# A fused GEGLU kernel: x of the second half transposed ahead of its use and kept in DRAM, wd sums staged in the pairs alone

## The chip, the cores and the metric

One core of a Trainium2 chip runs the whole kernel. The metric is the device time of one execution in microseconds, as the median over runs; lower is better. The kernel before takes 554.97 us (12 runs, 553.82 to 557.05).

## What is computed

The inputs are `x` (1 x 2048 x 1024), `w_gate` and `w_up` (1024 x 3584) and `w_down` (3584 x 1024), all bf16; the output is bf16.

```python
def reference(x, w_gate, w_up, w_down):
    return (_gelu(x @ w_gate) * (x @ w_up)) @ w_down   # gelu: tanh form
```

## The kernel before

The 2048 rows of x are worked off in two halves of 1024 rows (`h` = 0 and 1). Each half has a gate and up stage, which fills `hT` (the products, transposed, 28 f tiles of 128), and a down stage of two groups of 512 rows.

Most matrix products are not done plainly. Two by two blocks are multiplied in seven products instead of eight, from sums of blocks (a Strassen-Winograd scheme). In the gate and up stage, a *pair* (`pair_quads`) takes two f tiles and the half's two row blocks: its seven products, each for gate and up, are called m1, m5, m6, m2, m3 and two that are named by their sums s4 and a22, in this order, with 8 matmuls each, 56 in all. They need sums of x blocks (`t_sum`: t1, t2, t3, b22, t4, in `t_mem`, once in a half) and sums of weight blocks (`s_sum`, L350 on GpSimd, made for the next pair while the present one runs, in `s_mem`). Between the products VectorE adds (`add_m5`, L399) and multiplies gelu and up (`mult`, L255, which writes `hT`), and ScalarE copies banks and takes gelu. The first 512 columns of f of the first half are done plainly instead, in eight *units* (`first_units`, `unit`, L232). After the units come twelve pairs in the first half (pairs 2 to 13) and fourteen in the second. Weights of gate and up lie in two buffers of 512 columns each; `load_w` (L155) fills the next one at the start of every even pair, when the pair before has left it.

In the down stage (`down_group`), each of the four groups does seven products in the order m1, m5, m6, m7, m2, m3, m4 (28 matmuls each, L600). Their right side needs sums of blocks of w_down. t1 and t3 are made on VectorE from loaded rows, b22 on ScalarE, and t2 and t4 come ready from DRAM (`t_dram`, loaded at L520 in 512 KB pieces, as slots in `t_mem` come free). These two were *staged*: during the first half's gate and up stage, `stage_load` (L534) loads two rows of tiles of w_down into `wd_sb` (three buffers), and `stage_sums` makes three subtractions on VectorE (L548) into three `o_sb` tiles and stores two of them to `t_dram` (L552). There are 14 such steps. `o_sb` has four buffers. The b21 blocks are loaded at L496.

x must lie transposed in SBUF (`xT`, one buffer). The first half's is made on TensorE (first 512 rows) and by one DMA transpose (L172, `load_xT`). The second half's is loaded in the first half's down stage by 16 DMA transposes of 512 rows x 128 columns (128 KB each): six and four in group 0 behind m5 and m6, six in group 1 behind m5. In group 1 `w_fill` (L830) also brings the second half's first weights.

What sets the order: the helpers `sp`, `act`, `dve`, `pool`, `pe` tie each instruction to the one before it on its engine, so every engine runs in the order of the program text. Nearly all DMAs are issued by SyncE (`sp`), in one queue; a DMA that must wait there holds those behind it. Where `then["m2"]` and the like are filled, the listed work is issued behind that product of the pair or group. The lines that place the staging before:

```python
            stage_load(0)
            stage_load(1)
            unit(hT, (0, 0), 0, 1)
...
            for fi in range(1, FPG):
                stage_sums(fi - 1)
                stage_load(fi + 1)
                unit(hT, (0, 0), fi, 1)
...
                if i + 2 < NS:
                    then["m2"] = [lambda i=i: stage_load(i + 2)]
                if i < NS:
                    then["m4"] = [lambda i=i: stage_sums(i)]
```

Of the kernel before, what the change touches and what calls it, by code (L numbers as in the profile page):

```python
# [10 lines left out]
BF16 = mybir.dt.bfloat16  # L11
# [20 lines left out]
def kernel(  # L32
# [8 lines left out]
    nc = tc.nc  # L41
    P = 128
# [4 lines left out]
    KD = D // P  # L47
    KH = KD // 2
    KF = F // P
    TB = 512  # L50
    NH = 2
    SH = S // NH
    NTB = SH // TB
    FG = 512
    FPG = FG // P
# [6 lines left out]
    WKP = 2  # L62
# [5 lines left out]
    NS = KF // 2  # L68
# [5 lines left out]
    xv = x2.rearrange("t (ko ki) -> t ko ki", ki=P)  # L74
# [10 lines left out]
    o_pool = ctx.enter_context(tc.tile_pool(name="o", bufs=4))  # L85
    dram_pool = ctx.enter_context(
        tc.tile_pool(name="dram", bufs=1, space=bass.MemoryType.DRAM)
    )
# [11 lines left out]
    assert NR * DN == 5 * KH * TB and NS - 4 >= 2 * KD // 2  # L100

    t_dram = dram_pool.tile([P, 2, NS, DN], F32, name="t_dram")

    banks = [psum.tile([P, TB], F32, name=f"bank{i}") for i in range(8)]
    PB, VB, QB, RB = (0, 1), (2, 3), (4, 5), (6, 7)
# [18 lines left out]
    def sp(inst):  # L124
        return on("sp", inst)
# [43 lines left out]
    def load_xT(xT, h, tb, k0, k1):  # L169
        t0 = h * SH + tb * TB  # L170
        sp(
            nc.sync.dma_start_transpose(  # L172
                out=xT[:, k0:k1, tb * TB : (tb + 1) * TB],
                in_=xv[t0 : t0 + TB, k0:k1, :],
            )
        )
# [353 lines left out]
    def stage_load(i):  # L530
        w = wd_pool.tile([P, WDT, D], BF16, name="wd_sb")
        for j in range(2):
            k = j * NS + i
            sp(nc.sync.dma_start(out=w[:, j : j + 1, :], in_=wdv[:, k : k + 1, :]))  # L534
        staged[i] = w

    def stage_sums(i):
        w = staged[i]

        tt = [o_pool.tile([P, DN], F32R, name="o_sb") for _ in range(3)]  # L540
        ops = (
            (w[:, 0, DN:D], w[:, 0, 0:DN]),
            (w[:, 1, DN:D], tt[0][:].bitcast(F32)),
            (w[:, 1, 0:DN], tt[1][:].bitcast(F32)),
        )
        for t, (in0, in1) in zip(tt, ops):
            dve(
                nc.vector.tensor_tensor(out=t[:], in0=in0, in1=in1, op=ALU.subtract)  # L548
            )
        for j in range(2):  # L550
            sp(
                nc.sync.dma_start(  # L552
                    out=t_dram[:, j, i, :], in_=tt[1 + j][:].bitcast(F32)
                )
            )

    def s_down(hT, grp, name, i0, i1):
        n = 0 if name in ("s1", "s2", "s4") else 1
        for i in range(i0, i1, 2):
            t = left(n, i, i + 2)  # L560

            def a(l, j):
                c0 = grp * TB + l * 2 * P
                return hT[:, j * NS + i : j * NS + i + 2, c0 : c0 + 2 * P]

            if name == "a22":
                act(nc.scalar.copy(out=t, in_=a(1, 1)))
                continue
            in0, in1, op = {
                "s1": lambda: (a(1, 0), a(1, 1), ALU.add),  # L570
                "s2": lambda: (t.bitcast(F32), a(0, 0), ALU.subtract),
                "s3": lambda: (a(0, 0), a(1, 0), ALU.subtract),
                "s4": lambda: (a(0, 1), t.bitcast(F32), ALU.subtract),
            }[name]()
            dve(nc.vector.tensor_tensor(out=t, in0=in0, in1=in1, op=op))  # L575
# [167 lines left out]
    for h in range(NH):  # L743
        hT = hT_pool.tile([P, KF, SH], BF16, name="hT")
        first_pair = 0
        if h == 0:
            first_units(hT)
            t_sum("t2")
            for fi in range(NSU, FPG):
                unit(hT, (0, 0), fi, 0)  # L750
            t_sum("b22")
            t_sum("t3")
            stage_load(0)
            stage_load(1)
            unit(hT, (0, 0), 0, 1)
            for name in S_NAMES:
                for j in range(2):
                    s_sum(0, PPG, j, name)
            t_sum("t4")
            for fi in range(1, FPG):  # L760
                stage_sums(fi - 1)
                stage_load(fi + 1)
                unit(hT, (0, 0), fi, 1)
            first_pair = PPG
        for pair in range(first_pair, NPAIR):
            if pair % PPG == 0 and (pair // PPG + 1) * PPG < NPAIR:
                key = (h, pair // PPG + 1)
                if key not in chunks:
                    new_chunk(key)
                    load_w(key, 0, KD, nc.sync)  # L770
            then = {}
            if h == 0:
                i = pair - first_pair + FPG - 1
                if i + 2 < NS:
                    then["m2"] = [lambda i=i: stage_load(i + 2)]
                if i < NS:
                    then["m4"] = [lambda i=i: stage_sums(i)]
            if pair == NPAIR - 2:

                load_wd_rows(0, 4)  # L780
                load_wd_rows(4, 8)
            if 6 < pair < 11:
                i = 2 * pair - 8
                then["m3"] = [lambda i=i: s_down(hT, 0, "s3", i, i + 2)]
            if pair == NPAIR - 1:
                load_b22(4, 10)
                load_b22(10, NS)
                then |= {
                    "m5": [lambda: s_down(hT, 0, "s1", 0, 4)],
                    "m6": [lambda: s_down(hT, 0, "s1", 4, 8)],  # L790
                    "m2": [
                        lambda: load_wd_rows(8, 10),
                        lambda: load_wd_rows(10, 12),
                        lambda: load_wd_rows(12, NS),
                        lambda: load_b22(0, 4),
                    ],
                    "m7": [lambda: t_down(0, "t1", 0, 2)],
                    "m3": [lambda: t_down(0, "t1", 2, 4)],
                    "m4": [
                        lambda: t_down(0, "t2", 0, NT2),  # L800
                        lambda: t_down(0, "t1", 4, 8),
                        lambda: s_down(hT, 0, "s1", 8, NS),
                        lambda: t_down(0, "t1", 8, NS),
                    ],
                }
            pair_quads(
                hT, h, pair, (h, pair + 1) if pair + 1 < NPAIR else None, then
            )

        then0 = {"m5": [lambda: s_down(hT, 0, "s3", 0, 6)]}  # L810
        then1 = {}
        if h + 1 < NH:
            nh = h + 1
            xT = xT_pool.tile([P, KD, SH], BF16, name="xT")
            slices = [(tb, kd) for tb in range(NTB) for kd in range(KD)]

            def x_fill(n):
                fs = []
                for _ in range(n):
                    tb, kd = slices.pop(0)  # L820
                    fs.append(lambda tb=tb, kd=kd: load_xT(xT, nh, tb, kd, kd + 1))
                return fs

            def w_fill(c, j):
                if j == 0:
                    new_chunk((nh, c))
                w_sb, wv = chunks[(nh, c)][j], (wgv, wuv)[j]
                for k0 in range(0, KD, KH):
                    src = wv[:, k0 : k0 + KH, c * FG : (c + 1) * FG]
                    sp(nc.sync.dma_start(out=w_sb[:, k0 : k0 + KH, :], in_=src))  # L830

            def s_fill(j, *names):
                for name in names:
                    s_sum(nh, 0, j, name, True)

            then0["m5"] += x_fill(6)
            then0["m6"] = x_fill(4)
            then1["m5"] = x_fill(6)
            then1["m6"] = [lambda: w_fill(0, 0)]
            then1["m7"] = [lambda: w_fill(0, 1)]  # L840
            then1["m3"] = [
                lambda: t_sum("t1"),
                lambda: s_fill(0, "s1", "s2"),
                lambda: s_fill(1, "s1", "s2"),
            ]
            then1["m4"] = [
                lambda: s_fill(0, "a22"),
                lambda: s_fill(1, "a22"),
                lambda: t_sum("b22"),
                lambda: t_sum("t2"),  # L850
                lambda: t_sum("t3"),
                lambda: s_fill(0, "s3"),
                lambda: s_fill(1, "s3"),
                lambda: s_fill(0, "s4"),
                lambda: s_fill(1, "s4"),
                lambda: t_sum("t4"),
                lambda: [w_fill(1, j) for j in range(2)],
            ]
        for grp, then in enumerate((then0, then1)):
            down_group(hT, h, grp, then)  # L860
# [30 lines left out]
```

## Time and profile before

| what | value |
|---|---|
| median of 12 runs | 554.97 us |
| the profiled execution's own time | 554.39 us |
| its span | 552.6 us |
| TensorE busy | 540.2 us, 98% |
| VectorE, ScalarE, GpSimd busy | 350.6, 259.6, 243.6 us |
| DMA moved | 100.61 MB, mean 182 GB/s |
| units and start, to the first pair | 0 to 35.66 us |
| pairs of the first half | 35.66 to 193.28 us |
| its down groups | 193.28 to 239.60 to 284.68 us |
| pairs of the second half | 284.68 to 461.08 us |
| its down groups | 461.08 to 505.03 to about 549.1 us |

The profile is of one execution. PE is TensorE, DVE is VectorE, ACT is ScalarE, POOL is GpSimd, SPq is SyncE's queue of DMA issues; L376 is line 376 of the kernel. A row of a group of instructions ends with the engine's idle time ahead of them and what ended most of it, behind an arrow. A row in order of time begins with its start and its length, both in us; matmuls overlap, so a start and a length may reach into the next row. A row of a stretch has its bounds, its length, then busy time and number of instructions of PE, weight loads, DVE, ACT and POOL, then the clock that TensorE was granted (1.00 is full), the share of time that the DMA engines were busy, and the GB/s that they moved. "To landing" is the time from a DMA's issue until its data is there.

### The profile page before, as it was taken

The page shows a single profiled execution, that of the slowest core. Times are in us where ns is not written, and L with a number is a line of the kernel's source. Part 1 is how long each engine was busy: PE and PEld are TensorE (multiplying, and loading weights), DVE is VectorE, ACT ScalarE, POOL GpSimd, SP SyncE. Part 2 cuts the span into 40 slices and gives each one's busy share as a digit, 9 for nine tenths or more (in the row PEclk, how much of TensorE's full clock was granted, in tenths as well). Part 3 has the DMA queues.
Part 4 walks back from the last instruction along what each step waited for, and adds up shares of the span by engine and source line. Part 5 has one row for each costly group of instructions (what it writes and reads, how often), then busy time and mean ns, then how long its engine had stood idle before and what let it go on. Part 6 is the DMA issues. An engine that isn't in the chain of part 4 may idle for free.

```text
span 552.6 us, 7231 instructions
## 1 busy us (share of the span) xinstructions
PE 540.2 (98%) x2409; PEld 374.2 (68%) x2409; DVE 350.6 (63%) x465; ACT 259.6 (47%) x434; POOL 243.6 (44%) x206
## 2 busy tenths in 40 slices
PE   8969999999999999999999999999999999999997
PEld 4426677767777767658666777776777666866865
DVE  1893665566666899779394444444444459979861
ACT  2414555555555516313655555555555552361270
POOL 0476667777777000000019777777677740000000
PEclk9998999999999999999999999999999999999999
DMA  9848272737435689869990404224040447867846
GB/s 274 259 146 273 77 230 100 251 98 238 134 134 188 230 301 222 273 223 315 316 348 1 152 20 133 87 67 148 5 153 0 154 131 237 279 198 258 282 143 204
DMA packets 78788, 100.61 MB, mean 182 GB/s; under 512 B 16288, under 2 KB 60832, under 8 KB 78752
## 3 DMA queue, kind: packets, MB, share of 16 engines
q1 hardware_dynamic: 78208, 99.63, 55.9%
q10 hardware_dynamic: 544, 0.52, 0.3%
q8 instruction: 19, 0.31, 0.2%
q14 instruction: 17, 0.14, 0.1%
HBM read 85.46 MB, written 11.53 MB: 176 GB/s over the span
## 4 chain that ended last, share of the span: by engine, by line
PE 92%; DMA 5%; DVE 2%; issue 0%; SPq 0%; ACT 0%; ACTq 0%; DVEq 0%
PE bank L376 59%; PE bank L600 29%; DMA t_mem<-t_dram 3%; PE bank L232 3%; DMA w_mem<-in_w_up_dram 1%; DVE o_sb L548 1%; DMA wd_sb<-in_w_down_dram 1%; DVE t_mem L226 0%; DVE hT L255 0%; PE bank L294 0%; ACT o_sb L648 0%; ACTq L155 0%; SPq L534 0%; SPq L552 0%; DVEq L548 0%
## 5 line engine op out<-in xcount | busy, mean ns | idle before, releaser
L376 PE MATMUL bank<-t_mem,s_mem 128*128 128x512 f32 x1040 | 256.2, 401 | 0.0
L376 PEld LDWEIGHTS bank<-t_mem,s_mem 128*128 128x128 f32 x1040 | 196.3, 189 | 45.6 <-issue 0.3
L350 POOL TENSOR_TENSOR s_mem<-w_mem 128x512 fp32r<-128x512 bf16 x100 | 123.0, 1251 | 204.5 <-PE bank L376 185.1
L600 PE MATMUL bank<-t_mem,s_mem 128*128 128x512 f32 x560 | 131.6, 394 | 2.0 <-DMA t_mem<-t_dram 1.8
L399 DVE TENSOR_TENSOR bank<-bank,m 128x512 f32<-128x512 f32 x104 | 72.3, 699 | 93.0 <-ACT bank L419 83.7
L600 PEld LDWEIGHTS bank<-t_mem,s_mem 128*128 128x128 f32 x560 | 104.7, 188 | 26.7 <-issue 4.4
L376 PE MATMUL bank<-xT,w_mem 128*128 128x512 bf16 x416 | 99.8, 383 | 4.6 <-DVE hT L255 4.6
L255 DVE TENSOR_TENSOR hT<-w_mem,bank 128x512 bf16<-128x512 f32 x104 | 71.3, 687 | 50.5 <-ACT w_mem L250 26.3
L250 ACT ACTIVATE w_mem<-bank 128x512 f32<-128x512 f32 x104 | 61.7, 596 | 79.5 <-DVE bank L399 46.0
L376 PEld LDWEIGHTS <-w_mem 128*128 128x128 bf16 x416 | 36.6, 98 | 55.6 <-issue 18.8
L525 DVE TENSOR_TENSOR t_mem<-w_mem 128x1024 fp32r<-128x1024 bf16 x56 | 65.5, 1217 | 0.0
L350 POOL TENSOR_TENSOR s_mem<-w_mem,s_mem 128x512 fp32r<-128x512 bf16 x50 | 62.7, 1274 | 0.0
L350 POOL TENSOR_TENSOR s_mem<-s_mem,w_mem 128x512 fp32r<-128x512 f32 x50 | 59.4, 1211 | 0.0
L363 ACT CAST s_mem<-w_mem 128x512 fp32r<-128x512 bf16 x52 | 31.9, 615 | 29.9 <-PE bank L376 29.2
L575 DVE TENSOR_TENSOR s_mem<-hT 128x512 fp32r<-128x512 bf16 x56 | 36.6, 685 | 9.1 <-PE bank L600 7.0
L600 PEld LDWEIGHTS <-hT 128*128 128x128 bf16 x224 | 21.2, 98 | 26.7 <-issue 2.1
L414 ACT COPY m<-bank 128x512 f32<-128x512 f32 x52 | 30.6, 588 | 17.9 <-PE bank L376 17.8
L410 ACT COPY bank<-bank 128x512 f32<-128x512 f32 x52 | 29.5, 571 | 19.0 <-PE bank L376 19.0
L419 ACT COPY bank<-bank 128x512 f32<-128x512 f32 x52 | 29.6, 570 | 17.1 <-PE bank L376 17.1
L648 ACT CAST o_sb<-bank 128x512 bf16<-128x512 f32 x28 | 15.3, 584 | 42.4 <-PE bank L600 30.4
L232 PE MATMUL bank<-xT,w_mem 128*128 128x512 bf16 x128 | 28.1, 379 | 0.4 <-DMA w_mem<-in_w_up_dram 0.2
L522 ACT CAST t_mem<-w_mem 128x1024 fp32r<-128x1024 bf16 x28 | 26.9, 1047 | 0.0
(37 smaller groups left out, 225.5 us busy)
## 6 DMA issues: line engine op xcount, KB each, us to landing
t_mem<-t_dram SPq DMA_DIRECT2D x56, 512.0 KB, 5.9
w_mem<-in_w_gate_dram SPq DMA_DIRECT2D x11, 1024.0 KB, 5.6
w_mem<-in_w_up_dram SPq DMA_DIRECT2D x11, 1024.0 KB, 8.1
wd_sb<-in_w_down_dram SPq DMA_DIRECT2D x28, 256.0 KB, 5.6
t_dram<-o_sb SPq DMA_DIRECT2D x28, 256.0 KB, 2.1
wd_sb<-in_w_down_dram SPq DMA_DIRECT2D x12, 512.0 KB, 8.7
w_mem<-in_w_down_dram SPq DMA_DIRECT2D x10, 512.0 KB, 6.6
w_mem<-in_w_down_dram SPq DMA_DIRECT2D x4, 1024.0 KB, 7.1
```

The lines of the kernel that those rows point to most:

```text
L232: return nc.tensor.matmul(ps[:], lhsT=w_sb[:, kd, fi * P : (fi + 1) * P], rhs=xT[:, kd, tb * TB : (tb + 1) * TB], start=(kd == 0), stop=(k ...
L250: act(nc.scalar.activation(out=g_sb, in_=ps[:], func=ACT.Gelu_apprx_tanh))
L255: nc.vector.tensor_tensor(out=hT[:, fc, tb * TB : (tb + 1) * TB], in0=g_sb, in1=ps[:], op=ALU.mult,)
L350: pool(nc.gpsimd.tensor_tensor(out=t, in0=in0, in1=in1, op=op))
L363: act(nc.scalar.copy(out=t, in_=a(1, 1)))
L376: nc.tensor.matmul(banks[bank][:], lhsT=lhs[:, c, :], rhs=rhs[:, c, :], start=start and c == 0, stop=c == KH - 1, skip_group_check=True,)
L399: nc.vector.tensor_tensor(out=banks[dst][:], in0=banks[src][:], in1=m5[j][:], op=ALU.add)
L414: act(nc.scalar.copy(out=m5[j][:], in_=banks[VB[j]][:]))
L419: act(nc.scalar.copy(out=banks[RB[j]][:], in_=banks[QB[j]][:]))
L525: dve(nc.vector.tensor_tensor(out=t, in0=in0, in1=in1, op=ALU.subtract))
L575: dve(nc.vector.tensor_tensor(out=t, in0=in0, in1=in1, op=op))
L600: nc.tensor.matmul(banks[bset[u]][:], lhsT=lhs(i, u), rhs=rhs(i), start=start and i == 0, stop=stop and i == NS - 1, skip_group_check=True,)
```

## The change

It has three parts. The 14 staging steps no longer begin in the units: step 0 is loaded at their end, and the steps run behind pairs 2 to 12, four in every three pairs, so that behind some pairs two steps follow each other. In pairs 2 to 9, behind m5, two pieces of the second half's x are transposed by DMA into an `o_sb` tile each and stored to a new tensor in DRAM, `x_dram` (`stage_x`). In the down stage of the first half the 16 transposes are gone; behind m6 of group 0, four plain loads of 512 KB bring `xT` from `x_dram`.

```diff
+    x_dram = dram_pool.tile([P, KD, SH], BF16, name="x_dram")
...
+    def stage_x(tb, kd):
+        t0 = SH + tb * TB
+        t = o_pool.tile([P, 1, TB], BF16, name="o_sb")
+        sp(
+            nc.sync.dma_start_transpose(
+                out=t[:], in_=xv[t0 : t0 + TB, kd : kd + 1, :]
+            )
+        )
+        sp(
+            nc.sync.dma_start(
+                out=x_dram[:, kd : kd + 1, tb * TB : (tb + 1) * TB], in_=t[:]
+            )
+        )
...
-            stage_load(0)
-            stage_load(1)
             unit(hT, (0, 0), 0, 1)
...
             for fi in range(1, FPG):
-                stage_sums(fi - 1)
-                stage_load(fi + 1)
                 unit(hT, (0, 0), fi, 1)
             first_pair = PPG
+            xs = [(tb, kd) for tb in range(NTB) for kd in range(KD)]
+            stage_load(0)
...
             if h == 0:
-                i = pair - first_pair + FPG - 1
-                if i + 2 < NS:
-                    then["m2"] = [lambda i=i: stage_load(i + 2)]
-                if i < NS:
-                    then["m4"] = [lambda i=i: stage_sums(i)]
+                at = [min((pair - first_pair + d) * 4 // 3, NS) for d in range(3)]
+                then["m5"] = [lambda q=q: stage_x(*q) for q in xs[:2]]
+                xs = xs[2:]
+                then["m2"] = [lambda i=i: stage_load(i) for i in range(at[1], at[2])]
+                then["m4"] = [lambda i=i: stage_sums(i) for i in range(at[0], at[1])]
...
-            def x_fill(n):
-                fs = []
-                for _ in range(n):
-                    tb, kd = slices.pop(0)
-                    fs.append(lambda tb=tb, kd=kd: load_xT(xT, nh, tb, kd, kd + 1))
-                return fs
+            def x_fill(k0, k1):
+                src = x_dram[:, k0:k1, :]
+                sp(nc.sync.dma_start(out=xT[:, k0:k1, :], in_=src))
...
-            then0["m5"] += x_fill(6)
-            then0["m6"] = x_fill(4)
-            then1["m5"] = x_fill(6)
+            then0["m6"] = [
+                lambda k0=k0: x_fill(k0, k0 + WKP) for k0 in range(0, KD, WKP)
+            ]
```

More of the change, by code (lines that the diff above doesn't have):

```diff
@@ L814 @@
             xT = xT_pool.tile([P, KD, SH], BF16, name="xT")
-            slices = [(tb, kd) for tb in range(NTB) for kd in range(KD)]
-            def x_fill(n):
-                fs = []
-                for _ in range(n):
-                    tb, kd = slices.pop(0)
-                    fs.append(lambda tb=tb, kd=kd: load_xT(xT, nh, tb, kd, kd + 1))
-                return fs
+            def x_fill(k0, k1):
+                src = x_dram[:, k0:k1, :]
+                sp(nc.sync.dma_start(out=xT[:, k0:k1, :], in_=src))
             def w_fill(c, j):
```

## The prediction

> **What bounds the kernel now.** I read the page first (busy shares and clock), then TensorE's order of time, then VectorE around TensorE's one long gap, then SyncE's queue and the two down stages beside each other.
>
> ```profile
> PE 540.2 (98%) x2409; PEld 374.2 (68%) x2409; DVE 350.6 (63%) x465; ACT 259.6 (47%) x434; POOL 243.6 (44%) x206
> ...
> PEclk9998999999999999999999999999999999999999
> ...
> L600 PE MATMUL bank<-t_mem,s_mem 128*128 128x512 f32 x560 | 131.6, 394 | 2.0 <-DMA t_mem<-t_dram 1.8
> ...
> L376 PE MATMUL bank<-xT,w_mem 128*128 128x512 bf16 x416 | 99.8, 383 | 4.6 <-DVE hT L255 4.6
> ```
>
> TensorE is the bound. Only what stops it or slows its clock can be won, and the page names two such places: 4.6 us ahead of a gate/up matmul, and 1.8 us of t loads in the down stages. The dip in the clock row (fourth slice, 41 to 55 us) stands right behind the first. This is VectorE there, and the clock in four stretches:
>
> ```profile
> 28.56 1.64 DVE L548 TENSOR_TENSOR o_sb<-wd_sb 128x512 fp32r<-128x512 bf16 x1
> 30.23 3.09 DVE L548 TENSOR_TENSOR o_sb<-wd_sb,o_sb 128x512 fp32r<-128x512 bf16 x2
> 33.24 0.67 DVE L255 TENSOR_TENSOR hT<-w_mem,bank 128x512 bf16<-128x512 f32 x1
> ...
> 40.59 0.68 DVE L255 TENSOR_TENSOR hT<-w_mem,bank 128x512 bf16<-128x512 f32 x1
> ```
> ```profile
> 36.70:41.30 4.60, 0.00 (x0) 0.00 (x0) 4.50 (x6) 0.57 (x1) 0.78 (x1) 1.00 0.61 199
> 41.30:43.20 1.90, 1.88 (x5) 0.94 (x5) 0.00 (x0) 0.00 (x0) 0.00 (x0) 0.51 1.05 383
> 43.20:45.50 2.30, 2.30 (x8) 1.78 (x8) 0.00 (x0) 1.15 (x2) 0.54 (x1) 0.67 1.02 325
> 54.70:67.30 12.60, 12.60 (x58) 8.92 (x58) 7.53 (x11) 6.87 (x13) 9.21 (x9) 1.00 0.25 84
> ```
>
> Nine wd sums (L548), 1.5 us each while GpSimd works beside them, stand between the products (L255) of the last four plain units. The last product, which frees the bank of the first pair's second matmul group, comes at 40.59 instead of at about 35.9. TensorE stands from 36.7 to 41.3, and comes back at clock 0.51, then 0.67. An undisturbed pair takes 12.60 us; this first one takes 19.02 (35.66 to 54.68).
>
> The down stages, from SyncE's queue and TensorE:
>
> ```profile
> 206.39 17.41 SPq L172 DMA_TRANSPOSE xT<-in_x_dram  x10
> 223.92 1.46 SPq L520 DMA_DIRECT2D t_mem<-t_dram  x3
> ...
> 253.01 10.41 SPq L172 DMA_TRANSPOSE xT<-in_x_dram  x6
> ...
> 484.61 2.14 SPq L520 DMA_DIRECT2D t_mem<-t_dram  x3
> ```
> ```profile
> 234.15 2.18 PE L600 MATMUL bank<-t_mem,s_mem 128*128 128x512 f32 x7 [0.39 <-DMA t_mem<-t_dram]
> 237.90 1.86 PE L600 MATMUL bank<-t_mem,s_mem 128*128 128x512 f32 x7 [0.53 <-DMA t_mem<-t_dram]
> 283.00 1.84 PE L600 MATMUL bank<-t_mem,s_mem 128*128 128x512 f32 x7 [0.56 <-DMA t_mem<-t_dram]
> ```
>
> The ten transposes hold SyncE until 223.8, so the first t4 loads go out 30.6 us after their group began (193.28); in the same group of the second half, without transposes, 23.5 us after (461.08 to 484.61). From TensorE's order of time the four groups last 46.32, 45.08, 43.95 and about 44.0 us. The first half's two are 2.4 and 1.1 us longer, though one program text does all four.
>
> **The change, part by part.**
>
> *The sums leave the unit stage.* VectorE then has, behind the last t sum (26.18, 2.45 us), only products of 0.67 us, each ready when its unit's matmuls end. The last unit's end at 35.8, so its product is done at about 36.6, where TensorE asks at 36.55. The first pair costs 12.60 + 0.1 instead of 19.02: **−6.3 us**. What could be next late: GpSimd's s4 sums for that pair end at 37.46 and are needed 9 us after its start; weights of chunk 1 landed before 24. Neither waits. If the clock did not recover with the gap, only the 4.6 would be won. A rule of the Trainium skill bears on that (TensorE: Matmul & The Clock Gate, Part 1: The HAM clock gate): the half clock comes after some 3.4 us of idleness and needs about as long to go. The trace agrees (4.63 us of idleness; 0.51 and 0.67 until 45.5), so gap and slow clock go together: 4.6 by the gap alone, 6.3 with both; I take 6.3. The gaps of 0.33 to 0.56 us in the down stages stand at clock 1.00.
>
> *The transposes leave the down stages.* Group 0: SyncE issues the b21 loads to 206.35, then four loads of x of 512 KB, about 0.5 us of queue each, done by about 209, against 223.8. Their 2 MB follow 1.75 MB of b21; at 289 to 335 GB/s (these stretches' rates) both are through by about 217, when the first t4 loads may go (193.28 + 23.5). So group 0 falls to the second half's 43.95: **−2.3 us** (bounds 0 and −2.4). Group 1: w_fill's gate loads waited behind the transposes till 263.53; their slots are free when the t3 sums end at 260.3, so they go 3.2 us earlier. The last t4 load (issued 274.67, landed 8.2 us later) sat behind some 5.75 MB issued from 263.5 on, and was 0.56 us late; 3 us less backlog removes the wait: **−1.0** (bounds 0 and −1.1).
>
> *Sixteen transposes and stores enter the pairs.* Per pair, in eight pairs, SyncE's queue gets: transpose, store, transpose, store. A store waits for its transpose to land, and behind it stand the next transpose, the wd loads (L534) and the stores of the sums (L552). No row shows a transpose in the pairs. From the rows: standing alone one lands 2.7 us after issue (the last of the ten), 4.0 in the median of the 17, and 9.0 behind 1.75 MB, namely 0.5 after what was ahead of it; a store is 0.33 of queue and lands in 2.0. I take 2.7, and 0.5 behind a backlog, since in a pair each transpose stands alone but for the weights. Queue time over two pairs, 25.2 us: weights issued to first transpose landed 0.55 + 7.9 + 0.5 = 9.0; the other three transposes 9.0 (2.7 to 3.2 each); four stores 1.4; wd loads 2.5 (2.67 tiles of 0.95); stores of sums 2.0: 23.9. It fits, with 1.3 to spare. With 4.0 for the three it is 27, and the queue slips 2 us each two pairs.
>
> Here a rule speaks against the change (DMA: Bandwidth & Descriptors, Rules for kernel authors): make transfers of 1 MiB or more and join small ones. The trace's one large transpose (1 MB, landed in 8.1 us) beside eight small at 2.7 gives 21.6: joined pieces would need 16 us in all and no store between. By the row 16 × (2.7 + 0.35) = 49 us of queue are spent, but over 101 us of pairs in which SyncE now mostly waits for VectorE. The rule would price it at a slip; I keep the row's sum.
>
> *Who waits for a slip.* VectorE writes sums into the four o_sb slots that the transposes use too. Where a pair ends with two sums (first behind pair 4), the fifth of the six subtractions needs the slot of the second transpose, so its store must have landed. With P the start of pair 5: weights go out at 3.6 us into pair 4 (stores of the sums before end there), first transpose landed P + 0.1, store, second transpose P + 0.45 to 3.15, store issued 3.2, landed P + 5.25. Sums run from P + 1.05 (55.73 − 54.68) and would reach that one at 3.85; it starts at 5.3, both are done at 6.7, then add_m5 (L399) to 7.4. It starts at P + 5.34 today, and TensorE needs it only at P + 8.9 (s4 follows 40 matmuls). Margin 1.5 us, cost nothing; without that cover each later us is TensorE's. In the other even pairs the third subtraction needs the first transpose's store, about P + 2 to 4.5, limit P + 7.5. Weights may come 4 us later without GpSimd waiting: they land 9 and 12.2 us after the pair's start, it starts on them 15.5 after, and it is idle 3.4 of 12.6. Bounds of this part: 0 and +10; I take **+0.2**. A gain is excluded, since TensorE stands nowhere in these pairs.
>
> *The sums' new rate* (14 in 11 pairs): two sums are 4.2 us from P + 1.05, ending at 5.25 against the add's 5.34: nothing. Store and load of x are 4 MB more; DMA share in the pairs is 0.25 and 0.75: hidden.
>
> Sum: −6.3 − 2.3 − 1.0 + 0.2 = **−9.4 us**. The profiled execution took 554.39 (span 552.6), 0.6 below the median of 554.97: 545.0, and as a median **545.6**.
>
> **The rivals.** (A) *SyncE slips, a part is given back.* At 4.0 us a transpose the slip is 2 us each two pairs, 6 to 8 by the last transposes; after margins of 1.5 to 3 TensorE loses 2 to 6 us: 547.5 to 551.5. For it: the 4.0 median, the 9.0. Against it: that median comes from ones issued 1.3 us apart. Chance 0.22. (B) *Slower.* The same queue, in pairs 4 to 9: when those three transposes take 5 us each, two pairs' queue work is 30 us, the slip 4.7 each two pairs and 19 over the eight, less the margin of 3: 554.97 − 9.6 + 16 = 561. It decides from about 4.6 us per transpose (slip 3.4, 14 over the eight, less 3: 11), well above the 2.7 of the row. Chance 0.07. (C) *The down stages keep their waits* (x's 2 MB loads delay b21 or t4 as the transposes did): only −6.3 comes, 548.7. Against it: the same groups of the second half, and the idle DMA there. Chance 0.06. (D) *Nothing shows*, slips and gains equal, 555: 0.03. That it doesn't do what it says has no room: the built order has the transposes ahead of the wd loads and no L548 among the units.
>
> **How the numbers follow.** The likeliest case, 0.62, gives 544.6 to 546.8. The range goes to 550.5, into A, and leaves out B, D and A's end. Faster by over 0.2% (about what a measurement of this kernel can tell from no change) is the main case, A and C: 0.90; same 0.03; slower 0.07.
>
> **What would show it.** Right: no gap ahead of the first pair's second group, clock 1.00 from slice two on, pair 2 lasting 12.6 to 12.7; down groups of 44.0 and 44.1; the x transposes landing in 2.7, or 8 to 9 behind weights; L548's waits on DMA below 3 us each. Wrong: L399 ending waits of TensorE in pairs 5, 8 or 9, with VectorE waiting for x_dram<-o_sb (A, B), or t_mem<-t_dram still ending waits at L600 (C).

## The result, and the profile after

| | before | changed |
|---|---|---|
| median | 555.15 us (47 runs, 553.30 to 557.13) | 551.79 us (11 runs, 547.17 to 553.14) |
| ratio to before | | 0.992 (0.991 to 0.994) |
| the profiled execution, its span | 554.39, 552.6 us | 550.14, 548.1 us |

The change gains 3.4 us, where 9.4 were forecast (545.6), and lands above the range's upper end, 550.5. In a second set of runs the same kernel took 549.49 us (548.91 to 551.05; 0.990, 0.989 to 0.992). The lines of the page of the changed kernel that answer to those of before (the same code has other line numbers now: L548 is L549, L399 is L400, L376 is L377, L600 is L616):

```profile
PE 539.6 (98%) x2409; PEld 374.7 (68%) x2409; DVE 355.9 (65%) x465; ACT 259.3 (47%) x434; POOL 244.0 (45%) x206
...
PEclk9999999999999999999999999999999999999999
...
L377 PE MATMUL bank<-t_mem,s_mem 128*128 128x512 f32 x1040 | 255.9, 400 | 3.5 <-DVE bank L400 3.5
...
L616 PE MATMUL bank<-t_mem,s_mem 128*128 128x512 f32 x560 | 130.1, 393 | 0.0
...
L377 PE MATMUL bank<-xT,w_mem 128*128 128x512 bf16 x416 | 99.0, 381 | 0.0
```

Both waits named before are gone: L616 (down stages) stands 0.0, and so does the gate/up row that lost 4.6. The clock row has no dip left. But a third row has a wait that it did not have: 3.5 us for VectorE's add (L400). TensorE's order of time says where, as its last bracket (idle time ahead, and what ended it):

```profile
123.88 3.91 PE L377 MATMUL bank<-t_mem,s_mem 128*128 128x512 f32 x16 [2.08 <-DVE bank L400]
...
289.04 3.93 PE L377 MATMUL bank<-t_mem,s_mem 128*128 128x512 f32 x16 [1.39 <-DVE bank L400]
```

Those are the s4 products of pair 8 of the first half and of the first pair of the second half. From the same view, stage by stage:

| stage | before | changed | difference | forecast |
|---|---|---|---|---|
| start and units, to the first pair | 35.66 | 36.91 | +1.25 | 0 |
| first pair (pair 2) | 19.02 | 12.76 | −6.26 | −6.3 |
| pairs 3 to 13 | 138.60 | 140.96 | +2.36 | +0.2 |
| down group 0 | 46.32 | 43.94 | −2.38 | −2.3 |
| down group 1 | 45.08 | 43.95 | −1.13 | −1.0 |
| first pair of the second half | 12.60 | 14.29 | +1.69 | 0 |

The sum is −4.47, and the spans differ by 4.5. The gains all came at their forecast size (−9.77 against −9.6); the loss is three places that were priced at next to nothing. The first of them is the start: there the first 16 small transposes on TensorE took 1.89 us in this execution against 1.07 before. The second profile of the same kernel has 1.07 and reached its first pair at 35.55, and 1.89 comes again in two of the variants below, so that term belongs to the execution and not to the change.

**Pair 8** (its start P is 112.67). SyncE's queue in the pair before it; start, length of issuing, and what goes where:

```profile
106.54 1.88 SPq L535 DMA_DIRECT2D wd_sb<-in_w_down_dram  x4
...
109.41 1.98 SPq L563 DMA_TRANSPOSE o_sb<-in_x_dram  x1
114.50 0.32 SPq L568 DMA_DIRECT2D x_dram<-o_sb  x1
114.86 1.12 SPq L563 DMA_TRANSPOSE o_sb<-in_x_dram  x1
117.44 0.32 SPq L568 DMA_DIRECT2D x_dram<-o_sb  x1
```

Pair 6 issued the weights at 91.75, and its own first transpose, behind them, landed 11.4 us later (9.0 forecast). So the queue reaches pair 7's transposes late, and behind four wd loads (1 MB). The first lands 5.1 us after issue (109.41 to the store at 114.50), the second 2.6, and its store goes out only at P + 4.8. VectorE and GpSimd meanwhile:

```profile
116.36 0.92 DVE L549 TENSOR_TENSOR o_sb<-wd_sb,o_sb 128x512 fp32r<-128x512 bf16 x1 [1.24 <-DMA x_dram<-o_sb]
...
119.30 0.69 DVE L549 TENSOR_TENSOR o_sb<-wd_sb 128x512 fp32r<-128x512 bf16 x1 [2.02 <-DMA x_dram<-o_sb]
120.03 3.10 DVE L549 TENSOR_TENSOR o_sb<-wd_sb,o_sb 128x512 fp32r<-128x512 bf16 x2
120.98 3.16 POOL L351 TENSOR_TENSOR s_mem<-w_mem 128x512 fp32r<-128x512 bf16 x2
123.05 1.28 DVE L400 TENSOR_TENSOR bank<-bank,m 128x512 f32<-128x512 f32 x2
```

Two subtractions wait 1.24 and 2.02 us for the stores of x to give their slots back. The last two then take 1.55 us each, not 0.7, since GpSimd's sums run at the same time. The add starts at P + 10.4; TensorE's gap of 2.08 says that P + 8.3 was the latest that costs nothing. With 0.7 for the two it would have been 1.7 us earlier, a gap of some 0.4 (an estimate); without the 3.26 of waiting, in time: in the run without transposes, below, it starts at P + 7.8.

**First pair of the second half** (P is 278.52):

```profile
281.42 3.23 POOL L351 TENSOR_TENSOR s_mem<-w_mem 128x512 fp32r<-128x512 bf16 x2 [103.13 <-PE bank L377]
282.00 3.21 DVE L349 TENSOR_TENSOR s_mem<-w_mem,s_mem 128x512 fp32r<-128x512 bf16 x2
285.13 3.24 DVE L227 TENSOR_TENSOR t_mem<-xT,t_mem 128x2048 fp32r<-128x2048 bf16 x1
288.30 1.28 DVE L400 TENSOR_TENSOR bank<-bank,m 128x512 f32<-128x512 f32 x2
```

VectorE makes this half's first sums in one chain without idle time (t1, s1, s2, t2, t3, s3, s4, t4), which starts inside group 1. Before, it started 8.14 us ahead of the pair; the t4 waits of group 1 lay behind that start, so TensorE's waiting gave VectorE time. Now it starts 7.00 ahead. GpSimd's first sums for the next pair begin at P + 2.9 as ever, so in both kernels the chain's last pieces fall beside them. Before (P is 284.68), they began while VectorE was at s4, and it was GpSimd that waited:

```profile
287.01 1.28 DVE L348 TENSOR_TENSOR s_mem<-w_mem,s_mem 128x512 fp32r<-128x512 bf16 x2
287.58 5.05 POOL L350 TENSOR_TENSOR s_mem<-w_mem 128x512 fp32r<-128x512 bf16 x2 [106.64 <-PE bank L376]
288.22 2.28 DVE L226 TENSOR_TENSOR t_mem<-xT,t_mem 128x2048 fp32r<-128x2048 bf16 x1
```

Now they begin while VectorE is still at s3, and the two take turns: s4 takes 3.21 for two (1.28 before), t4 3.24 (2.28 before). No run here shows what settles who waits. 1.14 + 1.93 + 0.96 = 4.0 later: the add starts at P + 9.8 where it started at P + 5.7, and TensorE stands 1.39.

### The profile page after: what moved, and what is told of

Its sections match the earlier page's. It is cut to its first block, busy times and chain, and to the rows that moved or that the text cites. A ratio compares the mean times of both kernels' runs of the same rounds, so it can differ in the third digit from the quotient of the medians.

```text
span 548.1 us, 7258 instructions
## 1 busy us (share of the span) xinstructions
PE 539.6 (98%) x2409; PEld 374.7 (68%) x2409; DVE 355.9 (65%) x465; ACT 259.3 (47%) x434; POOL 244.0 (45%) x206
## 4 chain that ended last, share of the span: by engine, by line
PE 92%; DMA 4%; DVE 3%; issue 1%; SPq 0%; ACT 0%; DVEq 0%; ACTq 0%
PE bank L377 56%; PE bank L616 30%; PE bank L233 5%; DMA o_sb<-in_x_dram 1%; DVE s_mem L349 1%; DMA out_dram<-o_sb 1%; DMA w_mem<-in_x_dram 1%; PE bank L295 1%; DVE t_mem L222 0%; DVE o_sb L549 0%; DVE t_mem L224 0%; DVE bank L400 0%; DMA x_dram<-o_sb 0%; DVE t_mem L227 0%; ACT o_sb L664 0%
## 5 line engine op out<-in xcount | busy, mean ns | idle before, releaser
L377 PE MATMUL bank<-t_mem,s_mem 128*128 128x512 f32 x1040 | 255.9, 400 | 3.5 <-DVE bank L400 3.5
L377 PEld LDWEIGHTS bank<-t_mem,s_mem 128*128 128x128 f32 x1040 | 195.4, 188 | 49.4 <-issue 2.5
L351 POOL TENSOR_TENSOR s_mem<-w_mem 128x512 fp32r<-128x512 bf16 x100 | 119.3, 1213 | 198.7 <-PE bank L377 171.6
L616 PE MATMUL bank<-t_mem,s_mem 128*128 128x512 f32 x560 | 130.1, 393 | 0.0
L400 DVE TENSOR_TENSOR bank<-bank,m 128x512 f32<-128x512 f32 x104 | 71.6, 696 | 77.6 <-ACT bank L420 69.6
L616 PEld LDWEIGHTS bank<-t_mem,s_mem 128*128 128x128 f32 x560 | 105.2, 188 | 22.7
L377 PE MATMUL bank<-xT,w_mem 128*128 128x512 bf16 x416 | 99.0, 381 | 0.0
L377 PEld LDWEIGHTS <-w_mem 128*128 128x128 bf16 x416 | 36.5, 98 | 50.6 <-issue 13.4
L351 POOL TENSOR_TENSOR s_mem<-s_mem,w_mem 128x512 fp32r<-128x512 f32 x50 | 65.4, 1329 | 0.0
L351 POOL TENSOR_TENSOR s_mem<-w_mem,s_mem 128x512 fp32r<-128x512 bf16 x50 | 60.8, 1236 | 1.1 <-PE bank L377 1.1
L616 PEld LDWEIGHTS <-hT 128*128 128x128 bf16 x224 | 21.2, 98 | 26.7 <-issue 2.1
L549 DVE TENSOR_TENSOR o_sb<-wd_sb,o_sb 128x512 fp32r<-128x512 bf16 x28 | 24.6, 879 | 6.3 <-DMA x_dram<-o_sb 5.4
```

The lines of the kernel that those rows point to most:

```text
L351: pool(nc.gpsimd.tensor_tensor(out=t, in0=in0, in1=in1, op=op))
L377: nc.tensor.matmul(banks[bank][:], lhsT=lhs[:, c, :], rhs=rhs[:, c, :], start=start and c == 0, stop=c == KH - 1, skip_group_check=True,)
L400: nc.vector.tensor_tensor(out=banks[dst][:], in0=banks[src][:], in1=m5[j][:], op=ALU.add)
L616: nc.tensor.matmul(banks[bset[u]][:], lhsT=lhs(i, u), rhs=rhs(i), start=start and i == 0, stop=stop and i == NS - 1, skip_group_check=True,)
```

## The experiments

The theory behind them (Q): a slip of SyncE's queue reaches VectorE and, in pair 8, TensorE. Its rival (R): four steps in three pairs are too much for VectorE by themselves, since two sums behind one pair do not fit beside GpSimd. The kernel before took 555.1 to 555.7 us beside them.

**The changed kernel once more**, and with each half of it taken away. No edit in the first.

> The changed kernel once more. Its first profile (550.14 us) has two new waits of TensorE for add_m5 on VectorE: 2.08 us behind the two sums that follow pair 7, and 1.39 us in the second half's first pair; its granted clock is 1.000. Most other runs are 551 to 553 at a clock of 0.997. Theory Q (the queue slips, and sums that come late are slow) and rival R (two sums behind one pair are too much for VectorE whatever the queue does) both expect 551.8 +- 0.7 again. If the runs at 0.997 differ by a longer wait and a slow clock behind it, a profile at 0.997 shows a gap of over 2.1 us with clock near 0.5 behind it, worth some 1.7 us; if it is the start, the first pair begins later than at 36.9 instead.

549.49 us. Its profiled execution (550.38 us) shows the gap of pair 8 at another cost. Two stretches of it (columns as explained with the profile before):

```profile
120.02:123.44 3.42, 1.36 (x6) 0.86 (x5) 3.39 (x6) 0.00 (x0) 2.71 (x2) 1.00 0.56 199
123.44:126.85 3.41, 3.41 (x9) 2.64 (x8) 3.31 (x6) 1.08 (x2) 2.33 (x2) 0.50 0.99 322
```

TensorE stands 2.06 us (120.41 to 122.47), all of it within the first stretch, and through the next it has half the clock: the 16 matmuls behind the gap take 5.49 us. In the first profile of the changed kernel they took 3.91 behind a gap of 2.08 (121.80 to 123.88):

```profile
122.14:125.55 3.41, 1.67 (x7) 1.43 (x8) 3.41 (x6) 0.00 (x0) 2.36 (x3) 1.00 0.68 209
125.55:128.97 3.42, 3.42 (x17) 2.14 (x16) 3.31 (x6) 2.92 (x6) 1.96 (x2) 1.00 1.04 354
```

So the same gap costs 2.1 or 3.7 us. The bounds of these stretches are not chosen freely. In every profile here the half clock behind a gap lasts 3.41 us (twice that in one, the own slot below) and begins a whole number of such stretches after TensorE's clock first became full: 35 of them here, from 3.97 to 123.44. Counted on from 9.50, where the clock first became full in the first profile, a bound falls at 122.14, in the midst of that gap: 0.34 us of it lie ahead of the bound and 1.74 behind.

The other runs show the half clock in their mean clock. Of the changed kernel's first 12 runs, the profiled one included, 8 have 0.996 or 0.997 and took 551.26 to 553.14, and the four at 1.000 took 547.17 to 550.14; in the second set the two at 0.997 took 550.38 and 551.05, the three at 0.999 or 1.000 took 548.91 to 549.49. In the first set the two groups lie further apart (medians 552.1 and 548.3) than the 1.6 us of one stretch at half clock; the rest wasn't traced.

**No transposes in the pairs.** The second half's x is then loaded as many plain bytes, so its output is that of an x that is not transposed.

```diff
-                then["m5"] = [lambda q=q: stage_x(*q) for q in xs[:2]]
-                xs = xs[2:]
...
-                src = x_dram[:, k0:k1, :]
+                src = xplain[:, k0 * SH : k1 * SH].rearrange("p (a b) -> p a b", b=SH)
```

> No transposes and stores of x in the pairs; xT is loaded with as many bytes of x as they lie, so the second half's x is left untransposed. Q: SyncE has nothing to slip for, the sums behind pair 7 run at 0.7 us each from the pair's start on, no gap in the pairs; first pair -6.3, down groups 43.95 twice, 1.7 lost in the second half's first pair: 555.1 - 6.3 - 3.5 + 1.7 = 547.0. R: the gap of 2.1 us at pair 8 stays, near 549 to 552.

546.76 us (0.985, 0.983 to 0.986). Pair 8 (P is 111.39) has no gap; the only one left is the 1.39 in the second half's first pair. But its sums don't run at 0.7 us each, as expected: the last three of the six run beside GpSimd here too,

```profile
116.17 3.10 DVE L550 TENSOR_TENSOR o_sb<-wd_sb,o_sb 128x512 fp32r<-128x512 bf16 x2
```

and the add starts at 119.20, P + 7.8, only 0.5 us ahead of the latest that costs nothing. So the sums' new rate does no harm by itself, and R falls as the cause; but it uses up nearly all the time that VectorE had to spare.

**The sums alone**: staged in the pairs as in the change, while x is transposed in the down stage as before.

> The sums leave the units for the pairs, the transposes stay in the down stage as before. Q: -6.3 in the first pair and no other difference: 548.8; no gap in the pairs, down groups 46.3 and 45.1, and the second half's first pair 12.6, since TensorE comes to it 1.1 us later against VectorE's chain of sums. R: a gap of about 2 us behind each pair with two sums (pairs 4, 7, 10): 551 to 555.

547.47 us (0.987, 0.985 to 0.988), better than the whole change beside it (549.49, 0.990, 0.989 to 0.992). Its down groups last 45.07 and 45.3 (46.3 and 45.1 were expected, which is most of what it is below 548.8), and its second half's first pair 12.6. The two gaps of the changed kernel aren't there, only waits for t4 in the down groups, such as this one:

```profile
230.31 1.85 PE L616 MATMUL bank<-t_mem,s_mem 128*128 128x512 f32 x7 [0.52 <-DMA t_mem<-t_dram]
```

**x alone**: transposed in the pairs as in the change, while the sums stay in the units as before.

> The transposes and stores of x go into the pairs, the sums stay as before (three in the units, then one behind each pair). Q: the queue slips here too, but one sum needs only the first transpose's store, with a margin of 3 us or more: no gap in the pairs, the first pair still 19.0, down groups 43.95 twice, second half's first pair 14.3: 555.1 - 3.5 + 1.7 = 553.3. R expects the same. If the slip alone costs TensorE time, with one sum a pair, it is above 554.

553.69 us (0.998, 0.997 to 0.999). The 4.63 us gap of the first pair is back, with the clock behind it; both groups last 43.95; pair 8 has no gap, the second half's first pair has its 1.39. The queue slips less here than Q had expected: the weights go out 3.6 us behind the starts of pairs 4, 6 and 8 alike, and pair 7's stores of x 1.8 ahead of pair 8's start and 1.1 behind it, not 1.8 and 4.8 behind. So the slip of the changed kernel takes both, the transposes and two steps behind one pair. Moving x is worth 1.4 us when the sums stay where they were, and costs 2 us on top of the moved sums.

**Both stores behind m6**, so that the two transposes go out back to back and no store stands between them:

```diff
                 then["m5"] = [lambda q=q: stage_x(*q) for q in xs[:2]]
+                then["m6"] = [lambda q=q: store_x(*q) for q in xs[:2]]
```

> In each pair both transposes are issued behind m5 and both stores behind m6, so that the queue waits for landing once instead of twice: some 2 us less queue per pair. Q: the transposes of pair 7 are stored by 3 us into pair 8, its six subtractions end before VectorE's add is due, no gap there; the 1.4 us gap in the second half's first pair stays: near 546.8, as without transposes at all. If the gap at pair 8 does not come from the queue's slip, it stays, 549.5.

547.20 us (0.987, 0.985 to 0.989). SyncE's queue ahead of pair 8, which starts at 111.69 here:

```profile
103.48 4.56 SPq L565 DMA_TRANSPOSE o_sb<-in_x_dram  x2
110.55 0.80 SPq L573 DMA_DIRECT2D x_dram<-o_sb  x2
```

Both stores go out 1.1 us ahead of the pair, not 1.8 and 4.8 behind its start. The subtractions are as slow as before (the last two 3.10), but start in time: the add begins at 119.50, P + 7.8, and the gap is gone. Slow sums alone fit; only with the slip do they not. (The time alone would not show it: this interval touches that of the changed kernel's second set, 0.989 to 0.992.)

**The s4 sums of the second half's first pair on GpSimd**, to shorten VectorE's chain:

```diff
+                lambda: s_fill(0, "s4", on_dve=False),
+                lambda: s_fill(1, "s4", on_dve=False),
```

> For the second half's first pair the two s4 sums are made by GpSimd, idle until then, instead of VectorE. Theory: VectorE's chain of sums (t2, t3, s3, s4, t4) now ends late because group 1 ends 1.1 us earlier and because its last sums run beside GpSimd's first, at 1.6 us instead of 0.64 each. Two of the sums less: the add comes in time, the 1.4 us gap goes, that pair 12.6: 1.7 us less than the change, 547.8. If the gap comes of something else (a weight load, a bank), it stays.

553.88 us (0.996, 0.995 to 0.998), not what was expected: the gap grew to 2.11. VectorE and GpSimd there:

```profile
279.79 3.25 DVE L224 TENSOR_TENSOR t_mem<-xT 128x2048 fp32r<-128x2048 bf16 x1
281.76 3.86 POOL L351 TENSOR_TENSOR s_mem<-w_mem 128x512 fp32r<-128x512 bf16 x2 [0.87 <-PE bank L377]
282.96 3.21 DVE L349 TENSOR_TENSOR s_mem<-w_mem 128x512 fp32r<-128x512 bf16 x2
```

With GpSimd busy from ahead of the pair's start, t3 and s3 are slowed too (2.28 to 3.25, 1.28 to 3.21). Taking 1.28 us of work off VectorE cost it more than that. Both gaps of this profile were also followed by the half clock (5.50 and 5.47 us for 16 matmuls; mean clock 0.993), and much of the loss is that: its three runs at 0.999 or 1.000 took 549.89 to 550.86.

**The last two edits together.**

> Both edits. If both causes are as supposed they add: no gap left in the pairs, 545.2, which is the forecast's 545.6. If one gap only moves to the next thing that is late, it stays above 546.5.

548.50 us (0.989, 0.987 to 0.990). Pair 8's gap is gone, the 2.11 stays, and in this profile the matmuls behind it took 3.94.

**An own slot for the pieces of x**, so that VectorE's subtractions never wait for a store of x:

```diff
-        t = o_pool.tile([P, 1, TB], BF16, name="o_sb")
+        t = x_pool.tile([P, 1, TB], BF16, name="x_sb")
```

> The pieces of x get one small buffer of their own, so the sums never wait for a store of x, but each transpose now waits for the store of the one before: the queue slips more than in the change (some 1.7 us a transpose). If VectorE gets the slip through the shared slots, its waits for x_dram<-o_sb go and the gap at pair 8 goes or shrinks, near 547 to 548. If the slip reaches TensorE by late weights or late stores of the sums, the gap is longer than in the change: 551 or more.

555.74 us (1.000, 0.998 to 1.002): all of the gain is lost. With one slot the second transpose waits for the first's store, and the queue slips further. VectorE's waits (total, times, longest) name other transfers now:

```profile
PE bank L378 <- DVE bank L401: 7.8, 4, 5.4
...
DVE o_sb L550 <- DMA wd_sb<-in_w_down_dram: 6.6, 4, 3.0
DVE o_sb L550 <- DMA t_dram<-o_sb: 5.7, 3, 2.6
```

The wait for x_dram is gone, and the wd loads and the stores of the sums, which stand behind the transposes in the queue, came late instead: TensorE stands 5.4 us at pair 8. So the shared slots are only one way for the slip to reach VectorE; without them it comes by others.

**The first half's weights issued behind the transposes**, so that these don't wait behind 2 MB:

```diff
-                    load_w(key, 0, KD, nc.sync)
+                    if h == 0:
+                        late_w = [lambda key=key: load_w(key, 0, KD, nc.sync)]
...
+                then["m5"] = [lambda q=q: stage_x(*q) for q in xs[:2]] + late_w
```

> In the even pairs of the first half the weights of the next chunk (2 MB) are issued behind the pair's transposes and stores instead of ahead of them, so no transpose stands 8 us behind them. Theory Q: this takes 6 us of queue from every second pair, the slip ends, no gap at pair 8; GpSimd may wait a little for the weights: near 546.9 (the gap of 1.4 us in the second half's first pair stays). If the slip came from the transposes themselves and not from the weights ahead of them, the gap stays, 549.5.

552.00 us (0.993, 0.991 to 0.995), no gain over the change. Pair 7's transposes meet the weights instead:

```profile
100.56 2.83 SPq L535 DMA_DIRECT2D wd_sb<-in_w_down_dram  x4
...
104.90 1.14 SPq L563 DMA_TRANSPOSE o_sb<-in_x_dram  x1
113.71 0.32 SPq L568 DMA_DIRECT2D x_dram<-o_sb  x1
```

The weights went out at 99.50 and 100.05, 1 MB of wd behind them, then the transpose, which landed 8.8 us after issue. The gap at pair 8 is 2.60 (with the half clock behind it, 5.50), and pair 11 has one of 1.27. The bulk in front of a transpose was moved, not removed.

**The second half's t4 sum behind the first adds**, out of the chain ahead of s4:

```diff
+            if h == 1 and pair == 0:
+                then["m6"] = [lambda: t_sum("t4")]
```

> The second half's t4 sum moves on VectorE from ahead of the first pair's first two adds to behind them. Theory: the adds end 3.2 us earlier, the gap of 1.39 us ahead of s4 goes; t4 is then needed 3.9 us later and ends about in time (a gap of 0 to 0.6 us ahead of a22): 1 to 1.7 us less than the change, 548.2 where the change takes 549.5. If VectorE is late by its total work and not by the order, a gap of 1.4 us appears at a22 instead.

550.92 us (0.992, 0.990 to 0.994), no gain over the change. The 1.39 ahead of s4 became 1.30 ahead of the next product, a22: VectorE is late by its whole work beside GpSimd, not by one misplaced sum.

**This and the stores behind m6.**

> Stores behind both transposes, and t4 behind the adds. Both remaining gaps gone or under 0.6 us: 545.5, the forecast of 545.6 for the change. Above 546.5 if one of them only moved.

546.93 us (0.985, 0.982 to 0.987): below both kernels, and as fast as the one without transposes in the pairs (546.76), but no faster than with the stores behind m6 alone (547.20, 0.985 to 0.989). Pair 8's gap is gone; the other has moved to a22, 1.25.

**All three of these edits** (stores behind m6, t4 behind the adds, weights behind the transposes).

> As the last, with the weights behind the transposes too: the queue's slip is gone twice over. 545.3; if late weights begin to cost, above the last one, 546 or more.

550.25 us (0.989, 0.987 to 0.992), slower than the last. The weights' new place makes a gap of 2.06 at pair 5.

## Why the prediction was wrong, point by point

**Right.** The first pair: 12.76 us against 12.70, with the gap and the slow clock gone together. Both down groups: 43.94 and 43.95 against 43.95 and 44.0 to 44.1, and the plain loads of x delayed nothing. Most transposes with nothing large ahead: 2.5 to 2.8 us against 2.7. One behind weights: 7.7 to 9.7 from its own issue against 9.0. Pair 5, the only one that was worked through: the second store landed at P + 5.4 against P + 5.25, and no gap. That it had none owes something to luck: its sums ran beside GpSimd too, and the add started at P + 7.9, not 6.7, where P + 8.3 is the latest.

**Wrong, the first term: "I take +0.2" for the transposes in the pairs.** It cost 2.36 us. Three things in its working failed. The queue's sum over two pairs, 23.9, is an average that pairs 8 and 9 come near (24.4 from weights to weights, with no wait for VectorE among them), but pairs 6 and 7 took 26.0 to the end of pair 7's second store alone, where that part of the sum is some 22: 11.4 instead of 9.0 to the first transpose's landing, and 10.2 instead of 9.0 for the other three, of which the one behind 1 MB of wd loads took 5.1, not "2.7 to 3.2". The margin of 1.3 was smaller than this spread. (A first transpose's 11.4 counts from the weights' issue, 1.8 of it until its own.) Next, the place: "Where a pair ends with two sums (first behind pair 4)" was worked for pair 5 alone; two sums come next behind pair 7, and pair 8 was put among "the other even pairs" with one. Last, 0.7 us for each subtraction, in "two sums are 4.2 us from P + 1.05, ending at 5.25 against the add's 5.34: nothing". Beside GpSimd it is 1.55, a number that stood in the prediction's own rows (the 1.5 of the units). With no transposes at all the six take 6.8 us, and the add starts at P + 7.8: of the 3 us between P + 5.3, where it starts with one sum, and P + 8.3, the two sums by themselves take 2.5, and 0.5 is left for any slip. The slip took 2.6 more, to P + 10.4. The runs without transposes and with the stores behind m6 show that the gap goes with the slip. A rule of the Trainium skill (SBUF — State Buffer, section "SBUF: two separate sides") would have warned of the last: VectorE with two SBUF inputs and GpSimd share a port pair, and who comes second waits for the other's whole instruction. The trace agrees in kind: in pair 8 the two take turns, 1.55 to 1.6 us each, against 0.64 to 0.7 for VectorE alone, though ahead of the second half, before the change, GpSimd's sum waited for more than one instruction of VectorE; and the add L400, with a bank as one input, keeps its 0.64 at 123.05 beside a busy GpSimd.

**Wrong, the second: nothing after group 1's −1.0.** "Where a stall goes, what is late next" was asked for the first pair and not here. The 1.13 us won in group 1 became 1.69 lost in the pair that follows, a net loss: VectorE's chain of sums lost 1.14 us of its start, and then its turns against GpSimd. The gap of 1.39 (or its remainder ahead of a22, or 2.11) stands in every profile with the shorter group 1, and not in the two with the old transposes in the down stage. That the shorter group brings it is shown so; the part of the turns is read from the traces alone.

**Wrong, the third: no clock cost for a short gap.** The rule that the prediction cites (the Trainium skill, TensorE: Matmul & The Clock Gate, Part 1: The HAM clock gate) names some 3.4 us of idleness, and neither the sum nor rival A priced the clock for a shorter gap. Over the profiles of the changed kernel and its variants, eight gaps of 2.06 to 2.60 us stand; five were followed by the half clock (5.47 to 5.50 us for 16 matmuls, not 3.91 to 3.94), three were not. Where the gap lies against the stretches of 3.41 us tells the two kinds apart. In the five, 2.06 to 2.27 us of the gap lay within one stretch; in the three a bound fell into the gap, and its larger part was 1.47 to 1.74. The gaps of 1.25 to 1.39 never brought the half clock (behind those that stand ahead of 16 matmuls, these took 3.92 to 3.98). So the measurement decides: on this kernel TensorE need not stand for 3.4 us, about 2 within one stretch are enough, and a gap of 2 us costs 2.1 or 3.7. By their mean clock, 10 of the changed kernel's 17 runs had a stretch at half clock.

Together: −9.8 + 2.4 + 1.7 = −5.7, and −4.1 with the half clock. The second set of runs measured 555.11 − 549.49 = 5.6. The first set, most of whose runs had the half clock, gained 3.4. Its profiled execution lost 1.25 more at the start, but whether its other runs did so wasn't traced; this rest stays open.

**The rivals.** A, given 0.22, named the mechanism, VectorE waiting for the stores of x and TensorE for VectorE's add, and "Wrong: L399 ending waits of TensorE in pairs 5, 8 or 9" is what the page showed. But A's price was also wrong: it wanted 4.0 us for each transpose and a slip that grows over eight pairs. The median was 2.8, and the slip came and went: the weights were issued 3.6, 4.3, 10.9 and 7.7 us behind the starts of pairs 4, 6, 8 and 10. Most of the 10.9 isn't even the transposes': without them it is 8.8, since the weights stand behind the four stores of two slow sums. The sign "L548's waits on DMA below 3 us each" held (2.54 at most) and still TensorE stood: two short waits and two slow sums add up. B did not come (its 5 us per transpose was reached by none but those behind bulk loads), nor C or D.

## What to carry to other kernels

A step put into a queue has to be followed through every place of the pattern in which its neighbours differ, not through the first and the sum alone: a small transfer that something waits for takes the landing time of whatever bulk stands ahead of it, and it is cheap to issue both transfers first and both dependent stores later. Work is priced by a row in which the neighbouring engine is as busy as it will be then, and one such row is not enough where another shows the neighbour waiting instead. When a stall of the bounding engine is taken away, ask which chain had used that stall as its time, and test the halves of a change alone: here one half (547.5) beat the whole (549.5).

## What the hardware showed that was not expected

- VectorE and GpSimd slow each other in sums of SBUF tiles: 128x512 from 0.64 to 1.55 us, 128x2048 from 2.28 to 3.25 on VectorE. Before the change, ahead of the second half, VectorE kept its 0.64 and 2.28 and GpSimd's first two sums took 5.05, not 2.3. Giving GpSimd 1.28 us of VectorE's work made VectorE later.
- A TensorE gap of 2.06 us was followed by 3.41 us at half clock in one execution of a kernel, and a gap of 2.08 by none in another of the same kernel. In these traces it goes by the part of the gap that lies within one of the clock's stretches of 3.41 us: with the clock full until then, 2.06 or more brought the half clock, 1.74 or less did not.
- A DMA transpose of 128 KB landed 2.6 us after issue alone, 5.1 behind 1 MB of loads and two stores, 3.9 to 5.0 behind 512 KB of loads and two stores (x alone), up to 9.7 behind 2 MB of weights and 8.8 behind weights and 1 MB.
